# Pairs of blocks of the first MLP product by seven products: linear attention and a GELU MLP on one Trainium2 core

## The chip, the cores and the metric

The kernel runs on one core of one Trainium2 chip. The metric is the device time of one execution in microseconds (us). Each kernel was run several times; the median is given. One execution of each was also recorded by the hardware profiler, and all stretches inside the kernel come from that record. The engines are PE (TensorE, matrix products), ACT (ScalarE), DVE (VectorE), POOL (GpSimd) and SP (SyncE, which here only issues DMAs). Each engine works through its own instructions in the order in which the program gives them.

## What is computed

```python
# attention: q, k, v are [4, 8, 768, 64]; lam has one decay per head
for b in range(nb):                                   # blocks of the sequence
    intra = (q_b @ k_b.T * Dmask) @ v_b               # Dmask[i, j] = lam ** (i - j) for i >= j, else 0
    inter = (q_b * lam_pow) @ kv_state
    out_b = intra + inter
    kv_state = lam_block * kv_state + (k_b * rev_pow).T @ v_b
# MLP on x = attention's output, as [3072 tokens, 512]
h = x @ w_in                                          # w_in [512, 2048]
g = 0.5 * h * (1 + erf(h / sqrt(2)))
out = g @ w_out                                       # w_out [2048, 512]
```

## The kernel before

**Chunks and groups.** The sequence of 768 is cut into 6 blocks of 128. With 4 batches this gives 24 chunks; chunk n is block n // 4 of batch n % 4. Four chunks (one block of all batches) make a group of 512 tokens. While PE works on the MLP of group g, the attention of the four chunks of group g + 1 is slipped in between. `xT[g]` holds a group's attention output, transposed, as `x_t` [128, 4, 512] in bf16, one 128-row slice per input block.

**Attention of a chunk.** `begin` takes the loaded q, k and v; from chunk 8 on they are transposed by DMAs that SP issues (L192, L193), and v is scaled on POOL (`decay_v`, L167). `scores` (L195) multiplies k with q into two PSUM tiles `sc_ps`, one per half of the heads, and `masked` (L206) multiplies each by the mask on DVE into `sc_m` (L208). `outputs` (L226) adds the state's part and the chunk's own part into `o_ps`, which is then copied to `x_t`: on ACT for chunks below 8 (L243), on DVE from chunk 8 on (L245). `next_state` (L210) makes the next state with two DVE passes, an addition into `tmp` (L222) and a multiplication (L223). The loads of q, k and v are issued on POOL (L67), which also scales v.

**The MLP of group 0** has its own order. `mm1` (L407) makes one h block: four matmuls of 512 columns over the four input slices into `h_ps`, and a GELU on ACT into `g_t` (L420). `mm2` (L425) multiplies `g_t` with `w_out`, in two pairs of token blocks; each of the four results is copied by ACT into `o_sb` (L434, tag `o_s` of the output pool) and stored by SP (L435). The attention of chunks 4 to 7 stands in its second half: `transposes` on PE with ACT's copy of kT (L176), then `scores` and `outputs`.

**The MLP of groups 1 to 5.** The first stage is sixteen h blocks. The second stage is the product with `w_out`, done by seven products of halves in place of eight (`blocks_by_seven`, L271): `g_sum` (L280) builds five sums of halves of `g_t` on DVE, and m3, m4, m5, m2, m1, m6 and m7 each make one of the products, in two steps of eight matmuls of 256 columns (L310). Their results are combined on DVE and ACT into `o0` and `o1`, which SP stores (L320). In the last group the two halves of `r_ps` are two tiles, in banks of their own:

```python
if last:
    banks["r"] = [bank([128, DH], F32, tag, "r_ps") for tag in ("mh", "t")]
```

**PSUM.** There are eight banks. `bank` (L155) hands them out by tag: two each for `sc`, `mh` (h blocks, s, r) and `mo` (p, q and others), one each for `o` and `t`. A tile that gets the buffer of an earlier one waits until every reader of that one is done. The same holds for the pools in SBUF; `g_pool` and `out_pool` have two buffers per tag.

**The order.** It is written by hand: `tc.manual_schedule()` keeps the program's order on each engine. For groups 1 to 5 a list `todo` gives each attention step a place, counted in matmul columns (`place`, L547), and the loop at L598 runs a step before the first MLP block that begins at or behind its place.

Of the kernel before, what the change touches and what calls it, by code (L numbers as in the profile page):

```python
# [8 lines left out]
F32 = mybir.dt.float32  # L9
BF16 = mybir.dt.bfloat16  # L10
# [5 lines left out]
def kernel(  # L16
# [34 lines left out]
    g_pool = ctx.enter_context(tc.tile_pool(name="g", bufs=2))  # L51
    out_pool = ctx.enter_context(tc.tile_pool(name="outp", bufs=2))
# [55 lines left out]
    nc.vector.tensor_scalar(negj, pos, -1.0, None, op0=ALU.mult)  # L108
    dist = consts.tile([128, C], F32)
# [45 lines left out]
    def bank(shape, dtype, tag, name):  # L155
        return ps.tile(shape, dtype, tag=tag, name=name, bufs=2 if tag in ("sc", "mh", "mo") else 1)
# [38 lines left out]
    def scores(c):  # L195
        sc_ps = [bank([128, HP, C], F32, "sc", f"sc_ps{hi}") for hi in range(2)]
        for hp in range(HP):
            for hi in range(2):
                p = slice(hi * D, (hi + 1) * D)
                nc.tensor.matmul(sc_ps[hi][:, hp, :], c.kT[p, hp, :], c.qT[p, hp, :], start=True, stop=True)  # L200
        c.sc_m = work_pool.tile([128, HP, 2, C], BF16, tag="sc_m", name="sc_m")
        c.sc_ps = sc_ps
        for hi in range(2 if c.n > 0 else 0):
            masked(c, hi)

    def masked(c, hi):  # L206
        mask = decay[:, hi] if c.early else cmask[:, None, :].to_broadcast((128, HP, C))
        nc.vector.tensor_mul(c.sc_m[:, :, hi, :], c.sc_ps[hi], mask)  # L208

    def next_state(c):  # L210
        if c.sb == NB - 1:
            return
        kv_ps = bank([128, HP, 128], F32, "t", "kv_ps")
        for hp in range(HP):
            nc.tensor.matmul(kv_ps[:, hp, :], c.k[:, 2 * hp:2 * hp + 2, :], c.v_dec[:, 2 * hp:2 * hp + 2, :],  # L215
                             start=True, stop=True)
        new = work_pool.tile([128, HP, 128], BF16, tag="state_f", name="state", bufs=8)
        if c.sb == 0:
            nc.vector.tensor_mul(new, kv_ps, lam_blk)
        else:  # L220
            tmp = work_pool.tile([128, HP, 128], F32, tag="tmp", name="tmp")
            nc.vector.tensor_add(tmp, kv_ps, states[c.n])  # L222
            nc.vector.tensor_mul(new, tmp, lam_blk)  # L223
        states[c.n + M] = new

    def outputs(c, x_t, off, evacuate=True):  # L226
        o_ps = bank([128, HP, C], F32, "o", "o_ps")
        if c.sb > 0:
            for hp in range(HP):
                nc.tensor.matmul(o_ps[:, hp, :], states[c.n][:, hp, :], c.qT[:, hp, :],  # L230
                                 start=(hp == 0), stop=False, skip_group_check=True)
        v = c.v if c.early else c.v_dec
        for hi in range(2):
            for hp in range(HP):
                nc.tensor.matmul(o_ps[hi * D:(hi + 1) * D, hp, :], v[:, 2 * hp + hi, :], c.sc_m[:, hp, hi, :],  # L235
                                 start=(c.sb == 0 and hp == 0), stop=True, skip_group_check=True)
        c.x_o, c.o_ps = x_t[:, :, off * C:(off + 1) * C], o_ps
        if evacuate:
            empty_outputs(c)
# [30 lines left out]

    def blocks_by_seven(g, g_t, first):  # L271

        last = g == NG - 1
        TH = M * C // 2
        lo, hi = slice(0, TH), slice(TH, 2 * TH)
        gsum = {}
        G_SUMS = {6: (0, hi, 0, lo, ALU.subtract), 1: (0, lo, KH, hi, ALU.add), 2: (0, hi, KH, hi, ALU.add),
                  5: (0, lo, KH, lo, ALU.add), 7: (KH, lo, KH, hi, ALU.subtract)}

# [8 lines left out]
        n4 = KH // 2  # L288

        def with_sums(i, run):  # L290
            def both():
                run()
                if 10 <= i < 15:
                    g_sum((5, 2, 1, 6, 7)[i - 10], 0)
            return both

        paired = [kf for k in range(KH) for kf in (k, k + KH)]
        blocks = [(with_sums(i, first[kf][0]), first[kf][1]) for i, kf in enumerate(paired)]
# [9 lines left out]
        def product(i, u, o, begin):  # L308
            for k in range(KH):
                nc.tensor.matmul(o, left[i](k, slice(u * C, (u + 1) * C)), right[i](k),  # L310
                                 start=(begin and k == 0), stop=(k == KH - 1), skip_group_check=True)
# [4 lines left out]

        def store(rows, us, cols):
            b = slice(rows * 2 + us.start, rows * 2 + us.stop)
            dst = out_r[g, :, b, cols]
            nc.sync.dma_start(dst, sb["o0" if rows == 0 else "o1"][:, us, cols])  # L320

        both, every = slice(0, 2), slice(0, d_model)

        def m3(u):
            if u == 0:
                banks["p"] = bank([128, 2, DH], F32, "mo", "p_ps")
            product(3, u, banks["p"][:, u, :], u == 0)
            if u == 1:
                nc.scalar.copy(tile_f("e"), banks["p"])
                g_sum(5, n4)  # L330

        def m4(u):
            if u == 0:
                banks["q"] = bank([128, 2, DH], F32, "mo", "q_ps")
            product(4, u, banks["q"][:, u, :], u == 0)
            if u == 0:
                g_sum(2, n4)
            else:
                nc.scalar.copy(tile_f("f"), banks["q"])

        def m5(u):
            if u == 0:
                banks["p5"] = bank([128, 2, DH], F32, "mo", "p5_ps")
                g_sum(1, n4)
            product(5, u, banks["p5"][:, u, :], u == 0)
            if u == 1:
                sb["o0"] = out_pool.tile([128, 2, d_model], F32, tag="o0", name="o0_sb")
                nc.vector.tensor_add(sb["o0"][:, :, d_hi], sb["e"], banks["p5"])
                nc.vector.tensor_sub(tile_f("x1"), sb["f"], banks["p5"])
                if last:  # L350
                    store(0, both, d_hi)

        def m2(u):
            if u == 0:
                banks["q2"] = bank([128, 2, DH], F32, "mo", "q2_ps")
            product(2, u, banks["q2"][:, u, :], u == 0)
            if u == 0:
                g_sum(6, n4)
            else:
                sb["o1"] = out_pool.tile([128, 2, d_model], F32, tag="o1", name="o1_sb")  # L360
                nc.vector.tensor_add(sb["o1"][:, :, d_lo], sb["f"], banks["q2"])
                nc.vector.tensor_sub(tile_f("x2"), sb["e"], banks["q2"])

        def m1(u):
            if u == 0:
                banks["s"] = bank([128, 2, DH], F32, "mh", "s_ps")
                if last:
                    banks["r"] = [bank([128, DH], F32, tag, "r_ps") for tag in ("mh", "t")]
                else:
                    r_ps = bank([128, 2, DH], F32, "mh", "r_ps")  # L370
                    banks["r"] = [r_ps[:, 0, :], r_ps[:, 1, :]]
                    banks["r_all"] = r_ps
            product(1, u, banks["r"][u], u == 0 or last)
            if u == 0:
                g_sum(7, n4)
            elif last:
                for w in range(2):
                    nc.vector.tensor_add(sb["x2"][:, w, :], sb["x2"][:, w, :], banks["r"][w])
            else:
                nc.vector.tensor_add(sb["x2"], sb["x2"], banks["r_all"])  # L380

        def m6(u):
            product(6, u, banks["s"][:, u, :], u == 0)
            if u == 1:
                nc.vector.tensor_add(sb["o1"][:, :, d_hi], sb["x2"], banks["s"])
                store(1, both, every)

        def m7(u):
            product(7, u, banks["r"][u], False)
            if last:  # L390
                nc.vector.tensor_add(sb["o0"][:, u, d_lo], sb["x1"][:, u, :], banks["r"][u])
                store(0, slice(u, u + 1), d_lo)
            elif u == 1:
                nc.vector.tensor_add(sb["o0"][:, :, d_lo], sb["x1"], banks["r_all"])
                store(0, both, every)

        blocks += [((lambda f=f, u=u: f(u)), KH * DH) for f in (m3, m4, m5, m2, m1, m6, m7) for u in range(2)]
# [3 lines left out]

    def mlp_blocks(g):
        T = M * C
        x_t = xT[g]
        g_t = g_pool.tile([128, NK2, T], BF16, tag="g", name="g_t")
# [139 lines left out]
    later = NK2 * 4 * M * C + 7 * 2 * KH * DH  # L545

    def place(at):  # L547
        g, f = int(at), at - int(at)
        return round(f * total) if g == 0 else round(total + (g - 1 + f) * later)
# [11 lines left out]
        14: [lambda: next_state(live[3])],  # L561
        e: [w_out_sums, lambda: decay_v(live[4], nc.vector)],
# [12 lines left out]
    for n in range(2 * M, NCH):  # L575
# [4 lines left out]
                 (place(g + (at + apart if i < M - 1 else 0.93)), -OUTPUTS, n)]  # L580
# [3 lines left out]
    def step(minus_kind, n):  # L584
# [10 lines left out]
        else:  # L595
            outputs(live[n], xT[n // M], n % M)

# [45 lines left out]
```

## Time and profile before

| | |
|---|---|
| median of 3 runs (lowest to highest) | 211.31 us (211.16 to 211.94) |
| the profiled execution's own time | 211.0 us |
| its span, first to last instruction | 209.2 us |
| granted PE clock, mean | 0.997 |
| PE busy | 200.2 us (96%) |
| DVE busy | 139.8 us (67%) |
| ACT busy | 82.8 us (40%) |
| POOL busy | 94.8 us (45%) |
| PE's share of the chain that ended last | 92% |

The chain is the sequence of work and waits followed back from the last instruction. A row of the groups gives the line, engine, operation and shapes, then the total busy time, the mean in ns, and the idle time of the engine just before, with what ended most of it. The time of a matmul in such a row includes its way through the array, so consecutive matmuls overlap; how fast PE goes on is read from the chain or from the starts.

### The profile page before, as it was taken

How to read it: one execution, taken by the hardware profiler on the slowest of the kernel's cores; microseconds unless marked ns; L12 is line 12 of the kernel's file. 1: busy time of each engine (PE TensorE's matmuls, PEld its weight loads, DVE VectorE, ACT ScalarE, POOL GpSimd, SP SyncE). 2: the span in 40 equal slices, each digit the busy share in tenths (PEclk: the TensorE clock that was granted, in tenths of full speed). 3: DMA queues.
4: the chain of work that ended last, by engine and by line, in shares of the span. 5: the costliest groups of instructions: out<-in, count | busy, mean ns of one | idle time of the engine just before them, and what ended most of it. 6: DMA issues, size and time to landing. Idle time of an engine off the chain costs nothing.

```text
span 209.2 us, 4108 instructions
## 1 busy us (share of the span) xinstructions
PE 200.2 (96%) x1687; PEld 129.7 (62%) x1705; DVE 139.8 (67%) x220; ACT 82.8 (40%) x151; POOL 94.8 (45%) x110
## 2 busy tenths in 40 slices
PE   6689999999999999999999999999999999999992
PEld 1346674456545688655688655688654688544882
DVE  2583436665568889688779689579678579223382
ACT  4696664223556410255420265420265420366200
POOL 8978963899999793399500394000100000000000
PEclk9999999999999999999999999999999999999998
DMA  3999999999999999699990599100651000500014
GB/s 87 178 187 178 198 206 192 154 213 163 172 187 125 155 156 141 191 141 160 161 66 0 202 137 185 20 13 3 211 106 37 3 0 3 200 0 0 3 50 150
DMA packets 102370, 24.78 MB, mean 118 GB/s; under 512 B 92880, under 2 KB 99536, under 8 KB 102352
## 3 DMA queue, kind: packets, MB, share of 16 engines
q0 software_dynamic: 78096, 13.24, 90.3%
q1 hardware_dynamic: 23216, 11.02, 24.2%
q10 hardware_dynamic: 1040, 0.26, 0.6%
q8 instruction: 13, 0.21, 0.4%
q14 instruction: 5, 0.04, 0.1%
HBM read 27.27 MB, written 6.29 MB: 160 GB/s over the span
## 4 chain that ended last, share of the span: by engine, by line
PE 92%; DMA 3%; DVE 2%; issue 1%; ACT 1%; SPq 0%; DVEq 0%
PE h_ps L416 40%; PE r_ps L310 9%; PE p_ps L310 9%; PE q_ps L310 8%; PE o_ps L430 7%; PE o_ps L235 4%; PE s_ps L310 4%; PE sc_ps L200 4%; DMA wide_kq<-in_k_dram 3%; PE kv_ps L215 2%; PE o_ps L230 2%; PE t_ps L173 2%; DVE sc_m L208 1%; PE idle_ps L475 1%; DVE decay L496 0%
## 5 line engine op out<-in xcount | busy, mean ns | idle before, releaser
L420 ACT ACTIVATE g_t<-h_ps 128x512 bf16<-128x512 f32 (+3 forms) x101 | 58.1, 576 | 78.4 <-PE h_ps L416 78.2
L416 PE MATMUL h_ps<-x_t,w_in_t 128*128 128x512 bf16 (+3 forms) x434 | 88.5, 348 | 0.7
L416 PEld LDWEIGHTS <-w_in_t 128*128 128x128 bf16 x448 | 39.5, 98 | 36.2 <-issue 0.7
L167 POOL TENSOR_TENSOR v_dec<-v_t,lam_m 128x512 bf16<-128x512 bf16 x23 | 24.6, 1076 | 47.3 <-PE kv_ps L215 44.4
L310 PEld LDWEIGHTS <-g_sum 128*128 128x128 bf16 x400 | 38.5, 98 | 5.1
L285 DVE TENSOR_TENSOR g_sum<-g_t 128x1024 bf16<-128x1024 bf16 x50 | 34.0, 725 | 11.2 <-ACT g_t L420 11.2
L208 DVE TENSOR_TENSOR sc_m<-sc_ps,cmask 128x512 bf16<-128x512 f32 x40 | 25.6, 680 | 2.0 <-PE sc_ps L200 2.0
L67 POOL DMA_DIRECT2D k_t<-in_k_dram x23 | 21.2, 920 | 2.1 <-DMA w_out_t<-in_moe_w_out_dram 1.8
L67 POOL DMA_DIRECT2D q_t<-in_q_dram x23 | 20.5, 893 | 2.2 <-DMA w_out_t<-in_moe_w_out_dram 2.2
L67 POOL DMA_DIRECT2D v_t<-in_v_dram x23 | 20.4, 889 | 1.7 <-DMA w_out_t<-in_moe_w_out_dram 1.7
L310 PE MATMUL r_ps<-w_sum,g_sum 128*128 128x256 bf16 x160 | 19.3, 273 | 0.0
L310 PEld LDWEIGHTS <-g_t 128*128 128x128 bf16 x160 | 15.3, 98 | 3.2
L245 DVE TENSOR_TENSOR x_t<-o_ps,lam_q 128x512 bf16<-128x512 f32 x16 | 11.0, 687 | 8.4 <-PE o_ps L235 8.4
L222 DVE TENSOR_TENSOR tmp<-kv_ps,state 128x512 f32<-128x512 f32 x16 | 11.0, 689 | 7.3 <-PE kv_ps L215 7.3
L223 DVE TENSOR_TENSOR state<-tmp,lam_blk 128x512 bf16<-128x512 f32 x16 | 15.5, 972 | 0.5
L430 PE MATMUL o_ps<-w_out_t,g_t 128*128 128x512 bf16 x61 | 14.8, 380 | 0.1
L200 PE MATMUL sc_ps<-qT,kT 64*128 64x128 bf16 x192 | 10.0, 222 | 0.7 <-DVE sc_m L208 0.3
L200 PEld LDWEIGHTS <-kT 64*128 64x128 bf16 x192 | 5.8, 95 | 7.1 <-issue 2.7
L475 PE MATMUL idle_ps<-idle 128*128 128x512 bf16 x24 | 9.1, 495 | 1.2 <-DVE idle L101 1.2
L310 PE MATMUL p_ps<-w_sum,g_t 128*128 128x256 bf16 x80 | 10.1, 273 | 0.0
L310 PE MATMUL q_ps<-w_sum,g_t 128*128 128x256 bf16 x80 | 9.7, 273 | 0.0
L310 PE MATMUL q_ps<-w_out_t,g_sum 128*128 128x256 bf16 x80 | 9.6, 273 | 0.0
(67 smaller groups left out, 169.2 us busy)
## 6 DMA issues: line engine op xcount, KB each, us to landing
out_dram<-o_sb SPq DMA_DIRECT2D x9, 512.0 KB, 3.0
k_t<-in_k_dram POOLq DMA_DIRECT2D x23, 128.0 KB, 6.6
q_t<-in_q_dram POOLq DMA_DIRECT2D x23, 128.0 KB, 6.6
v_t<-in_v_dram POOLq DMA_DIRECT2D x23, 128.0 KB, 6.6
w_in_t<-in_moe_w_in_dram POOLq DMA_DIRECT2D x8, 256.0 KB, 8.7
w_out_t<-in_moe_w_out_dram POOLq DMA_DIRECT2D x4, 512.0 KB, 10.4
out_dram<-o_sb SPq DMA_DIRECT2D x5, 256.0 KB, 5.3
wide_kq<-in_q_dram ACTq DMA_DIRECT2D x1, 256.0 KB, 4.7
```

The source lines that it names most:

```text
L67: nc.gpsimd.dma_start(raw[n, name], chunk_of(name, n))
L167: eng.tensor_mul(c.v_dec, c.v, lam_m[:, :, None].to_broadcast((128, H, D)))
L200: nc.tensor.matmul(sc_ps[hi][:, hp, :], c.kT[p, hp, :], c.qT[p, hp, :], start=True, stop=True)
L208: nc.vector.tensor_mul(c.sc_m[:, :, hi, :], c.sc_ps[hi], mask)
L222: nc.vector.tensor_add(tmp, kv_ps, states[c.n])
L223: nc.vector.tensor_mul(new, tmp, lam_blk)
L285: nc.vector.tensor_tensor(gsum[i][:, ks, :], g_t[:, ka + k:ka + k + n4, ta], g_t[:, kb + k:kb + k + n4, tb], op=op)
L310: nc.tensor.matmul(o, left[i](k, slice(u * C, (u + 1) * C)), right[i](k), start=(begin and k == 0), stop=(k == KH - 1), skip_group_check=True)
L416: nc.tensor.matmul(h_ps[:, k, lo:hi], w_in_t[:, ki, (kf + k) * 128:(kf + k + 1) * 128], x_t[:, ki, cols.start + lo:cols.start + hi], start ...
L420: nc.scalar.activation(g_t[:, kf:kf + ks, cols], h_ps, ACT.Gelu)
L430: nc.tensor.matmul(om[io], g_t[:, kf, io * C:(io + 1) * C], w_out_t[:, kf, :], start=(kf == 0), stop=(kf == NK2 - 1))
L475: nc.tensor.matmul(idle_ps[0], idle[:, :128], idle, start=True, stop=True)
```

## The change

The change has five parts.

1. In groups 1 to 5, three (group 1) or four (the others) pairs of h blocks, kf and kf + 8, are made by seven products of halves, with 256 columns each, in place of sixteen half products. `pair_by_seven` gives two steps, `first` and `second`, with other blocks between them. Five sums of parts of `w_in` are made once on DVE (`w_in_sums`), and four sums of parts of `x_t` in each group (`x_sums`). Each pair has two banks of tag `mo`, `c_ps` and `d_ps`; ACT copies out of them, POOL adds, DVE subtracts and adds, and ACT's GELU reads c and the sum t.
2. From chunk 8 on, the scores of both halves lie in one tile of two banks; ACT copies them to bf16 and DVE multiplies by a bf16 mask in place.
3. The state's multiplication goes to POOL for blocks 2 to 4 of the sequence.
4. The seven products with `w_out` are ordered anew (m3, m4, m3, m4, m1, m6, m5, m2, m7), the later ones add onto the banks of the earlier ones, and POOL forms a common sum y.
5. `g_t` is one buffer for all groups, and the output pool has one buffer per tag. The last outputs of a group stand at 0.9 of it, not 0.93.

The core of the diff (bodies that are only re-sorted are left out):

```diff
-    g_pool = ctx.enter_context(tc.tile_pool(name="g", bufs=2))
-    out_pool = ctx.enter_context(tc.tile_pool(name="outp", bufs=2))
+    g_pool = ctx.enter_context(tc.tile_pool(name="g", bufs=1))
+    out_pool = ctx.enter_context(tc.tile_pool(name="outp", bufs=1))
...
+    cmask_b = consts.tile([128, C], BF16)
+    nc.vector.tensor_copy(cmask_b, cmask)
...
     def scores(c):
-        sc_ps = [bank([128, HP, C], F32, "sc", f"sc_ps{hi}") for hi in range(2)]
+        sc_ps = bank([128, 2, HP, C], F32, "sc", "sc_ps")
...
-        for hi in range(2 if c.n > 0 else 0):
-            masked(c, hi)
+        if c.n >= 2 * M:
+            nc.scalar.copy(c.sc_m, sc_ps)
+            flat = c.sc_m.rearrange("p hi hp i -> p (hi hp) i")
+            nc.vector.tensor_mul(flat, flat, cmask_b[:, None, :].to_broadcast((128, H, C)))
+        else:
+            for hi in range(2 if c.n > 0 else 0):
+                masked(c, hi)
...
-            nc.vector.tensor_mul(new, tmp, lam_blk)
+            (nc.vector if c.sb == 1 else nc.gpsimd).tensor_mul(new, tmp, lam_blk)
...
+    PAIRS = {g: 3 if g == 1 else 4 for g in range(1, NG)}
...
+    def w_in_sums():
+        for i, (a, b, op) in W_IN_SUMS.items():
+            wisum[i] = w_pool.tile([128, 2, SW * 128], BF16, name=f"wi_sum{i}")
+            nc.vector.tensor_tensor(wisum[i], w_in_t[:, a[0], a[1]], w_in_t[:, b[0], b[1]], op=op)
...
+    def x_sums(g):
+        x_t = xT[g]
+        both = sum_pool.tile([128, NK1, TH], BF16, tag="xs67", name="x_sum67")
+        for i, pa, pb, op in ((4, (d1, t_lo), (d0, t_lo), ALU.subtract), (3, (d0, t_hi), (d1, t_hi), ALU.subtract),
+                              (1, (d0, t_lo), (d1, t_hi), ALU.add)):
+            xsum[i] = sum_pool.tile([128, 2, TH], BF16, tag=f"xs{i}", name=f"x_sum{i}")
+            nc.vector.tensor_tensor(xsum[i], x_t[:, pa[0], pa[1]], x_t[:, pb[0], pb[1]], op=op)
+        nc.vector.tensor_tensor(both, x_t[:, :, t_lo], x_t[:, :, t_hi], op=ALU.add)
+        xsum[6], xsum[7] = both[:, d0], both[:, d1]
...
+        def product(i, o, begin, end=True):
+            for ki in range(2):
+                nc.tensor.matmul(o, w[i][:, ki, :], x[i][:, ki, :], start=(begin and ki == 0), stop=(end and ki == 1),
+                                 skip_group_check=True)
+
+        def first():
+            sb["c"] = bank([128, 2, TH], F32, "mo", "c_ps")
+            sb["d"] = bank([128, 2, TH], F32, "mo", "d_ps")
+            product(4, sb["c"][:, 1], True)
+            product(3, sb["c"][:, 0], False)
+            zf = sum_pool.tile([128, 2, TH], F32, tag="h_zf", name="h_zf", bufs=2)
+            nc.scalar.copy(zf, sb["c"])
+            product(1, sb["d"][:, 0], True)
+            e = sum_pool.tile([128, TH], F32, tag="h_e", name="h_e", bufs=2)
+            nc.scalar.copy(e, sb["d"][:, 0])
+            product(6, sb["d"][:, 1], False)
+            y = sum_pool.tile([128, TH], F32, tag="h_y", name="h_y", bufs=2)
+            nc.gpsimd.tensor_add(y, zf[:, 0], zf[:, 1])
+            nc.gpsimd.tensor_add(y, y, e)
+            sb["y"] = y
+
+        def second():
+            product(5, sb["c"][:, 0], False)
+            product(2, sb["c"][:, 1], False)
+            t = sum_pool.tile([128, 2, TH], F32, tag="h_t", name="h_t", bufs=2)
+            nc.vector.tensor_sub(t, sb["y"][:, None, :].to_broadcast((128, 2, TH)), sb["c"])
+            nc.scalar.activation(halves[:, 2 * kf + 1:2 * (kf + KH) + 1:2 * KH - 1, :], sb["c"], ACT.Gelu)
+            product(7, sb["d"][:, 0], True)
+            nc.vector.tensor_add(t, t, sb["d"])
+            nc.scalar.activation(halves[:, 2 * kf:2 * (kf + KH) + 2:2 * KH + 1, :], t, ACT.Gelu)
+        return (first, 8 * TH), (second, 6 * TH)
...
-        paired = [kf for k in range(KH) for kf in (k, k + KH)]
-        blocks = [(with_sums(i, first[kf][0]), first[kf][1]) for i, kf in enumerate(paired)]
+        seven = [None] + [pair_by_seven(g, kf, g_t) for kf in range(1, PAIRS[g] + 1)]
+        if g == 1:
+            order = [0, 8, 5, 13, (1, 0), 6, (1, 1), 14, (2, 0), 4, (2, 1), 12, (3, 0), 7, (3, 1), 15]
+        else:
+            order = [0, (1, 0), 8, (1, 1), 5, (2, 0), 13, (2, 1), 6, (3, 0), 14, (3, 1), 7, (4, 0), 15, (4, 1)]
+        blocks = [seven[o[0]][o[1]] if isinstance(o, tuple) else first[o] for o in order]
+        blocks[-2] = then(blocks[-2], 1, 0)
+        blocks[-1] = then(blocks[-1], 6, 0)
...
+        early_k, late_k = (0, 5, 6, 7), (1, 2, 3, 4)
+        def m3(part):
+            if part == 0:
+                two("p", "mo")
+                product(3, each("p"), True, False, early_k)
+                g_sum(1, n4)
             else:
+                product(3, each("p"), False, True, late_k)
+                nc.scalar.copy(tile_f("z"), banks["p"])
+                g_sum(5, 0)
...
+        def m2(u):
+            product(2, each("q"), False, us=(u,))
+            if u == 1:
+                tile_o(1)
+                nc.vector.tensor_sub(sb[1][:, :, d_hi], sb["y"], banks["q"])
+                nc.vector.tensor_add(sb[1][:, :, d_hi], sb[1][:, :, d_hi], banks["s"])
+                nc.scalar.copy(sb[1][:, :, d_lo], banks["q"])
                 store(1, both, every)
...
+        steps = [(m3, 0), (m4, 0), (m3, 1), (m4, 1)] + [(f, u) for f in (m1, m6, m5, m2, m7) for u in range(2)]
...
+    g_t = g_pool.tile([128, NK2, M * C], BF16, name="g_t")
...
+        e - 3: [w_in_sums],
         e: [w_out_sums, lambda: decay_v(live[4], nc.vector)],
...
-                 (place(g + (at + apart if i < M - 1 else 0.93)), -OUTPUTS, n)]
+                 (place(g + (at + apart if i < M - 1 else 0.9)), -OUTPUTS, n)]
...
             outputs(live[n], xT[n // M], n % M)
+            if n % M == M - 1:
+                x_sums(n // M)
```

More of the change, by code (lines that the diff above doesn't have):

```diff
@@ L234, in outputs @@
             for hp in range(HP):
[L235 removed]
+                nc.tensor.matmul(o_ps[hi * D:(hi + 1) * D, hp, :], v[:, 2 * hp + hi, :], c.sc_m[:, hi, hp, :],
                                  start=(c.sb == 0 and hp == 0), stop=True, skip_group_check=True)
@@ new lines, in pair_by_seven @@
+    def pair_by_seven(g, kf, g_t):
+        x_t = xT[g]
+        own = lambda f: slice(f * 128, (f + 1) * 128)
+        w = {3: w_in_t[:, d0, own(kf)], 4: w_in_t[:, d1, own(kf + KH)]}
+        w.update({i: wisum[i][:, :, own(kf - 1)] for i in W_IN_SUMS})
+        x = dict(xsum)
+        x.update({2: x_t[:, d0, t_lo], 5: x_t[:, d1, t_hi]})
+        halves = g_t.rearrange("p kf (th t) -> p (kf th) t", th=2)
+        sb = {}
+        def product(i, o, begin, end=True):
[27 more added lines that the diff above has]
+        return (first, 8 * TH), (second, 6 * TH)
@@ L306, in blocks_by_seven, with product, two @@
         banks, sb = {}, {}
[L308 to L311, printed above, removed]
+        def product(i, o, begin, end=True, ks=range(KH), us=(0, 1)):
+            for k in ks:
+                for u in us:
+                    nc.tensor.matmul(o[u], left[i](k, slice(u * C, (u + 1) * C)), right[i](k),
+                                     start=(begin and k == ks[0] and u == us[0]), stop=(end and k == ks[-1]),
+                                     skip_group_check=True)
+        def two(name, tag):
+            banks[name] = bank([128, 2, DH], F32, tag, f"{name}_ps")
+            return banks[name]
+        each = lambda name: [banks[name][:, u, :] for u in range(2)]
         def tile_f(name):
@@ L353, in m2 @@
         def m2(u):
[L354 to L380, printed above, removed]
```

107 lines of the change are left out of this document (62 added, 45 removed).

## The prediction

> **What bounds the kernel now.** I read the page first: which engine is full, and when.
>
> ```profile
> PE 200.2 (96%) x1687; PEld 129.7 (62%) x1705; DVE 139.8 (67%) x220; ACT 82.8 (40%) x151; POOL 94.8 (45%) x110
> PE   6689999999999999999999999999999999999992
> ```
>
> PE is full from the third slice to the last. A change gains only if it shortens PE's stream and leaves PE waiting for nobody. Next, the chain of waits, once for group 2 and once for group 5, gives the stage before the w_out products.
>
> ```profile
> 86.12 0.22 PE h_ps L416
> ...
> 102.28 0.87 PE p_ps L310 x8
> ```
> ```profile
> 179.40 0.21 PE h_ps L416
> ...
> 193.29 1.75 PE p_ps L310 x16
> ```
>
> So that stage takes 16.16 us in group 2 (groups 3 and 4 alike) and 13.89 in group 5, which has no attention: 16 h blocks of 0.868. Sixteen 256-column matmuls take 1.75, 0.109 each. Group 1's stage, from the full chain, is 54.83 to 71.19: 16.36.
>
> Third, the groups by form, for what the new evacuations cost.
>
> ```profile
> L420 ACT ACTIVATE g_t<-h_ps 128x512 bf16<-128x512 f32 x86 | 51.4, 597 | 74.8 <-PE h_ps L416 74.8
> L329 ACT COPY f_e<-p_ps 128x512 f32<-128x512 f32 x5 | 2.9, 586 | 9.0 <-DVE sc_m L208 6.6 <-PE p_ps L310 2.3
> L420 ACT ACTIVATE g_t<-h_ps 128x256 bf16<-128x256 f32 x3 | 1.2, 384 | 0.1
> L167 POOL TENSOR_TENSOR v_dec<-v_t,lam_m 128x512 bf16<-128x512 bf16 x23 | 24.6, 1076 | 47.3 <-PE kv_ps L215 44.4 <-DMA v_t<-in_v_dram 2.4 <-PE h_ps L416 0.4
> ```
>
> Fourth, the timeline at two places, for the gaps between engines.
>
> ```profile
> 40.05 0.59 ACT L434 COPY o_sb<-o_ps 128x512 f32<-128x512 f32 x1 [5.45 <-PE o_ps L430]
> 40.67 1.22 SPq L435 DMA_DIRECT2D out_dram<-o_sb  x2
> 40.92 0.59 ACT L434 COPY o_sb<-o_ps 128x512 f32<-128x512 f32 x1 [0.28 <-PE o_ps L430]
> 41.40 0.59 ACT L176 COPY kT<-t_ps 128x512 bf16<-128x512 bf16 x1
> 42.18 0.40 PE L200 MATMUL sc_ps<-qT,kT 64*128 64x128 bf16 x8
> ```
> ```profile
> 54.87 0.59 ACT L243 CAST x_t<-o_ps 128x512 bf16<-128x512 f32 x1 [0.20 <-PE o_ps L235]
> 55.73 0.39 PE L215 MATMUL kv_ps<-v_dec,k_t 128*128 128x128 bf16 x4
> 55.95 0.59 PE L416 MATMUL h_ps<-x_t,w_in_t 128*128 128x512 bf16 x2
> 56.15 0.69 DVE L222 TENSOR_TENSOR tmp<-kv_ps,state 128x512 f32<-128x512 f32 x1 [1.75 <-PE kv_ps L215]
> ```
>
> ACT starts one 512-wide piece 0.48 after another (40.92, 41.40). A reader of PSUM starts 0.20 after PE has gone on (55.95, 56.15). An engine's result reaches the next engine in about 0.05 (DVE's qT ends at 42.13, the scores start at 42.18). DVE's state multiply, which needs tmp, starts 0.72 after it (58.97, 59.69).
>
> **The saving.** Each of 19 pairs (3 + 4x4) replaces two h blocks (1.736) by 14 matmuls (1.53): 0.21 each, 3.9 us.
>
> **What a pair waits for.** Call its halves A (`first`) and B (`second`). In A, ACT copies bank c (`zf`), then half of bank d (`e`); product 6 writes d's other half. No row of before shows a reader and PE in one bank: in group 5, where DVE reads one half of r_ps while PE writes the other, L368 puts them in two banks. So either product 6 waits for `e` or it doesn't. I take the wait, since `d_ps` is one tile of one bank. Likewise Gelu of c behind DVE's subtraction from c. From c's last matmul: 0.20 + 0.48 + 0.38 + 0.06 = 1.12 until product 6, where PE's own work is 0.22 (product 1).
>
> The Trainium skill, page "PSUM — Partial Sum Buffer", section "PSUM bank collisions raise a hardware error", says that no two engines may be in one bank and quadrant at once, two readers included. By it both waits are there, 256 us; without them it is the first rival, 233. The split r_ps agrees, but shows no wait.
>
> ACT, in order, then closes a ring: product 6 0.22, h block 0.87, products 5 and 2 0.44, gap 0.20, subtraction 0.72, addition 0.69, gap 0.05, Gelu of t 0.48, Gelu of the next h block 0.48, `zf` 0.48, `e` 0.38, gap 0.06: **5.07 us per pair**, where four blocks took 3.47. GpSimd's two adds make y beside it: at half of 1.08 each they end 0.59 + 0.05 + 1.08 = 1.72 after `zf` starts, and the subtraction starts at 2.65. At a full 1.08 each they come 0.2 late, 3.8 in all; cheaper adds gain nothing.
>
> Group 5: first block and A up to product 6: 0.87+0.44+0.20+0.48+0.38+0.06+0.22 = 2.65; three rings 15.21; then, since p_ps takes c's bank, block 15, products 5 and 2, gap, subtraction, Gelu of c and two gaps: 0.87+0.44+0.20+0.69+0.05+0.60+0.05 = 2.90. Sum 20.76, so +6.9.
>
> Groups 2 to 4 add attention. Two kv products on the ring's path: 0.44. The masks: ACT's copy of 1024, an estimate from 384 and 586 for 256 and 512, is 1.01, then DVE's multiply 0.60, both ahead of the subtraction. Scores ahead of h block 8: 0.33+0.20+1.01+0.05+0.60 = 2.19 instead of 1.51, +0.68; with outputs (0.57) ahead of block 14: +1.25. Sum 23.13 against 16.16: +7.0 each, **21.0**. Off the ring, the copy would be free.
>
> Group 1: four blocks and two kv 3.91, A 1.78, two rings 10.14, a kv 0.22, a score copy in ACT's queue 0.9, then 2.76 to the last subtraction and 1.39 to p_ps: 21.10 against 16.36, +4.7. Together the pair stages cost **32.6**, the saving included.
>
> **The output pool with one buffer.** Tag `o_s` has it too. Group 0's second output copy must wait until the first's store has landed:
>
> ```profile
> DMA to landing us min/median/max: 5.3/5.5/6.1
> ```
>
> 40.67 + 5.5 = 46.2. Behind it in ACT's queue is kT, at 46.7 to 47.2, and PE's scores for chunk 4 go from 42.18 to 47.3: 5.1 us. The other two copies do it again: the store of the third, issued near 53.4 + 5.1, lands at 64.0; behind the fourth is x_t of chunk 7 (54.87), which group 1's first h block needs: 65.1 instead of 60.6, 4.6 us. Together **9.7** (9.3 to 10.9 by the landings).
>
> PE then stands still for longer than it took to lose its clock at the end, where its last matmuls end near 205.5 (the windows; the column behind the busy times is the granted clock):
>
> ```profile
> 207.60:208.20 0.60, 0.00 (x0) 0.00 (x0) 0.00 (x0) 0.00 (x0) 0.00 (x0) 0.79 0.02 3
> 208.20:208.80 0.60, 0.00 (x0) 0.00 (x0) 0.00 (x0) 0.00 (x0) 0.00 (x0) 0.50 0.00 0
> ```
>
> At the start a 512 took 0.43 from 7.7 until about 10, then 0.22. Three us at half speed lose 1.5: **3.0** for two gaps (0 to 3.4).
>
> **What costs nothing.** w_in sums: five of 0.69 on DVE ahead of w_out's, where DVE waits 1.85 and 1.99 for w_out; uncovered, 3.4. x sums, 1.95 per group, have most of 2.6 us behind the last outputs; uncovered, up to 1.3. The mask copy hides in DVE's 4.2 us wait for k. State decay on GpSimd (near 1.08, row L167) is needed a group later; ahead of y it fits into 0.9 of slack. The loads (0.9 each) go out ahead of the next pair's adds. Outputs at 0.9 still stand before m7. g_t's single buffer is read by g_sums that m7 itself waits for. The w_out stage keeps its 112 matmuls; DVE's work there (eight g_sums 5.4, three x_t and two masks 3.5, four combinations 2.7, x sums 1.95: 13.5 of 14.9 us) stays ahead of the products, and a late g_sum would cost 0.68. The combinations in four steps save DVE three passes that were off PE's path; in the last group they put SP's store of o1 behind two DVE passes instead of one, 0.7 later, and its 3.0 us still land before the last store's (uncovered, 0.7).
>
> The Trainium skill, page "SBUF — State Buffer", section "Who interferes with whom", lets a DVE operation with two SBUF inputs contend with GpSimd's reads. L223 has two and took 0.69 to 1.39. By that rule eight masks could take 0.7 more each, 262 us. Subtraction and addition read PSUM and stay.
>
> **Sum.** 32.6 + 9.7 + 3.0 = 45.3 on the profiled execution's 211.0 (span 209.2, 1.8 around it; the median of 3 is 211.31): **256**.
>
> **Rivals.**
> 1. One bank is shared freely: no wait at product 6 or at Gelu of c. The ring becomes `zf` 0.59, gap, two adds 1.08, gap, 0.72, 0.69, gap, two Gelus 0.96: 4.19. Group 5 +2.7, groups 2 to 4 +2.0 each, group 1 +0.9, output pool 12.7: 233. For it: the halves are different addresses. 12%.
> 2. The output copies don't wait, though the pool says one buffer: 256 - 12.7 = 244. 7%.
> 3. Faster: evacuations stay hidden as Gelu is now (0.27 idle after each). It decides itself where ACT, GpSimd and DVE return both banks within a pair cycle's 3.27 us of PE work. Then 211.0 - 3.9 = 207. Against it: even the shorter ring is 4.19. 6%.
> 4. PE's clock falls in the pair stages, where it is busy 3.3 of 5.1 us: matmuls on the ring (1.53) double, 19 x 1.53 = 29, giving 285. Against it: no gap there reaches 2 us. 5%.
>
> The forecast has 70%, by itself 249 to 266 (dearer adds, contention; gaps a tenth shorter). The range reaches down to rival 1: 232 to 266. Measurement tells 0.5% from no change. Faster 0.05, same 0.01 (rest of rival 3), slower 0.94.
>
> **What would show it.** Right: PE idle before c_ps and d_ps, released by ACT's copy of `e` and Gelu of c; A some 2 us long; c_ps every 5 us; PE idle about 5 us near 42 and 4.6 near 60, behind o_sb's DMA; p_ps 20.8 us after group 5's first h block. Wrong: product 6 starting right behind product 1, kT right behind the second o_sb copy, or PE full through the pair stages.

## The result, and the profile after

The changed kernel takes **264.15 us** (median of 4 runs, 262.66 to 267.04) against 211.24 for the kernel before on the same chip: a ratio of 1.2472, 95% interval 1.2407 to 1.2537. The medians are of all runs, but the ratios leave out slow runs (here the one of 267.04), so that a ratio can differ a little from that of the medians. The profiled execution took 264.56, its span is 262.8. Line numbers below are those of the changed kernel, or of the experiment's, which differ by a few.

The page's busy totals and its row of slices for PE, and the clock granted to it:

```profile
PE 210.3 (80%) x1819; PEld 143.2 (55%) x1819; DVE 159.8 (61%) x240; ACT 120.8 (46%) x221; POOL 154.2 (59%) x170
...
PE   5899994798858898667899687599867599865893
...
PEclk9799999599989999999999979999979999999998
```

PE was full from the third slice on; now no h stage (the stage of the first MLP product) is, and the clock row dips at four places between the kernel's start and its end. PE's busy time is 10 us longer though its stream is shorter; part of it runs at half clock. GpSimd went from 94.8 us to 154.2.

The waits (engine, tile and line, what it waited for; us in total, times, longest):

```profile
PE d_ps L318 <- ACT h_e L330: 22.1, 19, 2.2
...
ACT o_sb L524 <- DMA out_dram<-o_sb: 7.7, 2, 5.6
PE c_ps L318 <- ACT g_t L342: 7.6, 13, 1.2
...
PE p_ps L391 <- ACT g_t L342: 6.5, 5, 1.6
PE sc_ps L202 <- ACT kT L178: 5.3, 2, 5.2
```

Product 6 waits for ACT's copy of `e` in each of the 19 pairs. In 13 of them the pair's first product waits for Gelu of the c of the pair before. The timeline of group 5 holds one whole ring, the closed loop of steps from one pair's subtraction to the next pair's (start, duration, engine, line, and in brackets the idle time before it and what ended it):

```profile
234.12 0.69 DVE L341 TENSOR_TENSOR h_t<-h_y,c_ps 128x512 f32<-128x512 f32 x1 [3.74 <-PE c_ps L318]
...
234.91 0.69 DVE L344 TENSOR_TENSOR h_t<-h_t,d_ps 128x512 f32<-128x512 f32 x1
...
235.63 0.63 ACT L345 ACTIVATE g_t<-h_t 128x512 bf16<-128x512 f32 x1 [0.19 <-DVE h_t L344]
...
236.64 0.58 ACT L327 COPY h_zf<-c_ps 128x512 f32<-128x512 f32 x1
237.11 0.39 ACT L330 COPY h_e<-d_ps 128x256 f32<-128x256 f32 x1
...
237.55 0.38 PE L318 MATMUL d_ps<-x_sum,wi_sum 128*128 128x256 bf16 x2 [1.24 <-ACT h_e L330]
...
239.33 0.69 DVE L341 TENSOR_TENSOR h_t<-h_y,c_ps 128x512 f32<-128x512 f32 x1 [3.74 <-PE c_ps L318]
```

From 234.12 to 239.33 is 5.21 us, of which PE's own work, at the spacing of its matmuls in the kernel before, takes 3.27. Subtraction, addition, Gelu of t, Gelu of the h block, `zf`, `e`, product 6, the h block, products 5 and 2: this is the ring that the prediction wrote down.

The timeline of group 0 shows the output pool's one buffer, at both places:

```profile
46.57 0.59 ACT L524 COPY o_sb<-o_ps 128x512 f32<-128x512 f32 x1 [5.60 <-DMA out_dram<-o_sb]
...
47.70 0.61 PE L202 MATMUL sc_ps<-qT,kT 64*128 64x128 bf16 x8 [5.18 <-ACT kT L178]
...
63.16 0.59 ACT L524 COPY o_sb<-o_ps 128x512 f32<-128x512 f32 x1 [2.12 <-DMA out_dram<-o_sb]
```

PE's first gap is 5.2 us, and the clock is at half from 46.0 to 52.8. At the second place the store had landed after 2.0 us, and PE lost 1.0.

Stage by stage, from the starts of the matmuls in the two traces: group 1's first h block comes 7.7 us later; the h stages of groups 1 to 5 are longer by 8.8, 8.2, 10.0, 9.6 and 7.4; group 1's w_out stage by 1.1; the end by 0.8. Together 53.6, the difference of the spans.

### The profile page after: what moved, and what is told of

Same layout as the page of the kernel before. It is cut to its first block, busy times and chain, and to the rows that moved or that the text cites. A ratio compares the mean times of both kernels' runs of the same rounds, so it can differ in the third digit from the quotient of the medians.

```text
span 262.8 us, 4592 instructions
## 1 busy us (share of the span) xinstructions
PE 210.3 (80%) x1819; PEld 143.2 (55%) x1819; DVE 159.8 (61%) x240; ACT 120.8 (46%) x221; POOL 154.2 (59%) x170
## 4 chain that ended last, share of the span: by engine, by line
PE 47%; ACT 14%; POOL 11%; DVE 11%; issue 10%; DMA 5%; SPq 0%; DVEq 0%; POOLq 0%; ACTq 0%
PE h_ps L506 13%; PE p_ps L391 5%; PE o_ps L520 5%; DVE h_t L341 5%; PE q_ps L391 4%; DVE h_t L344 3%; PE r_ps L391 3%; ACT h_zf L327 3%; PE d_ps L318 3%; POOL v_dec L169 3%; PE c_ps L318 3%; DMA out_dram<-o_sb 3%; ACT g_t L345 3%; PE o_ps L242 2%; DMA wide_v<-in_v_dram 2%
## 5 line engine op out<-in xcount | busy, mean ns | idle before, releaser
L506 PE MATMUL h_ps<-x_t,w_in_t 128*128 128x512 bf16 (+3 forms) x296 | 61.5, 344 | 1.4 <-ACT x_t L250 1.0
L510 ACT ACTIVATE g_t<-h_ps 128x512 bf16<-128x512 f32 (+3 forms) x63 | 35.2, 560 | 34.5 <-PE h_ps L506 34.3
L333 POOL TENSOR_TENSOR h_y<-h_zf 128x256 f32<-128x256 f32 x19 | 14.0, 735 | 45.8 <-ACT h_zf L327 45.8
L318 PE MATMUL d_ps<-x_sum,wi_sum 128*128 128x256 bf16 x114 | 22.4, 279 | 22.1 <-ACT h_e L330 22.1
L318 PEld LDWEIGHTS <-wi_sum 128*128 128x128 bf16 x190 | 19.1, 101 | 32.5 <-issue 27.1
L506 PEld LDWEIGHTS <-w_in_t 128*128 128x128 bf16 x296 | 25.5, 100 | 18.8 <-issue 4.1
L341 DVE TENSOR_TENSOR h_t<-h_y,c_ps 128x512 f32<-128x512 f32 x19 | 13.0, 685 | 27.2 <-PE c_ps L318 21.9
L206 ACT CAST sc_m<-sc_ps 128x1024 bf16<-128x1024 f32 x16 | 16.2, 1011 | 23.9 <-PE sc_ps L202 23.9
L230 POOL TENSOR_TENSOR state<-tmp,lam_blk 128x512 bf16<-128x512 f32 x12 | 15.3, 1271 | 17.3 <-DVE tmp L229 17.3
L342 ACT ACTIVATE g_t<-c_ps 128x512 bf16<-128x512 f32 x19 | 11.4, 598 | 18.5 <-DVE h_t L341 18.5
L208 DVE TENSOR_TENSOR sc_m<-sc_m,cmask_b 128x1024 bf16<-128x1024 bf16 x16 | 12.4, 776 | 12.2 <-ACT sc_m L206 12.2
L318 PE MATMUL c_ps<-x_sum,w_in_t 128*128 128x256 bf16 x76 | 11.4, 271 | 7.6 <-ACT g_t L342 7.6
L252 DVE TENSOR_TENSOR x_t<-o_ps,lam_q 128x512 bf16<-128x512 f32 x16 | 11.0, 685 | 10.6 <-PE o_ps L242 10.6
## 6 DMA issues: line engine op xcount, KB each, us to landing
w_out_t<-in_moe_w_out_dram POOLq DMA_DIRECT2D x4, 512.0 KB, 10.4
```

What stands on the lines that cost most here:

```text
L206: nc.scalar.copy(c.sc_m, sc_ps)
L230: (nc.vector if c.sb == 1 else nc.gpsimd).tensor_mul(new, tmp, lam_blk)
L318: nc.tensor.matmul(o, w[i][:, ki, :], x[i][:, ki, :], start=(begin and ki == 0), stop=(end and ki == 1), skip_group_check=True)
L333: nc.gpsimd.tensor_add(y, zf[:, 0], zf[:, 1])
L341: nc.vector.tensor_sub(t, sb["y"][:, None, :].to_broadcast((128, 2, TH)), sb["c"])
L506: nc.tensor.matmul(h_ps[:, k, lo:hi], w_in_t[:, ki, (kf + k) * 128:(kf + k + 1) * 128], x_t[:, ki, cols.start + lo:cols.start + hi], start ...
```

## The experiments

**1. Two output buffers.** The copies of group 0 use the two larger output tiles in turn (lines shortened at `...`):

```
-  o_sb = out_pool.tile([128, d_model], F32, tag="o_s", ...)
+  o_sb = out_pool.tile([128, 2, d_model], F32, tag=f"o{io % 2}", ...)[:, 0, :]
```

> Group 0's output copies take turns in two buffers (those of the later groups, which stand empty until then), everything else as after the change. Theory (the one buffer costs two gaps and PE's clock behind the first): the gap of 5.2 us ahead of the scores near 47.7 goes, so does the 1.0 us ahead of group 1's first h block, and the stretch at half speed behind the first gap (48.2 to 53, some 1.5 us); 264.2 falls by 7 to 8 us, to 256 to 257, and group 1's first h block comes near 55 instead of 62.4. Rival (the copies wait for something else, or the time is lost again in the pair stages): less than 3 us, 261 or more.

Measured: 253.59 us, 10.6 less (ratio to before 1.2027, 1.195 to 1.2103). Both waits are gone, and the first h block of group 1 comes at 55.70, 6.7 us earlier. The rest of the gain is in the h stages of groups 1, 3 and 4 (2.2, 1.8 and 1.4 shorter), where this execution had no stretch at half clock and the changed kernel's had one each; it had one in group 2, which is 1.1 longer. The 10.6 thus holds 6.7 from group 0 and a balance of half-clock stretches; why fewer of them came without the gaps isn't shown.

**2. No pairs.** `PAIRS` is 0 everywhere, all blocks plain, everything else as changed.

> All 16 h blocks of each group are plain again, in the order of the kernel before; the sums of w_in and of x are still made, and masks, state, combinations and the one output buffer stay as after the change. Theory (the pair stages cost 42 to 45 us, by the stage lengths of the trace: 8.8, 8.2, 10.0, 9.6 and 7.4, less what sums and masks cost by themselves): about 220 to 222, group 5's h stage 13.9 again, groups 2 to 4 near 16.2. Rival (masks on ACT, state on GpSimd and x sums are what stretches groups 2 to 4, and only group 5's 7.4 and group 1's part are the pairs'): 240 or more, with h stages of 20 or more in groups 2 to 4.

Measured: 232.19 us (1.0952, 1.0882 to 1.1023). Taking the pairs out gains 32.0 us, and the h stages of groups 2 to 4 are back at 16.16. So the rival is wrong on the h stages; but the time is 10 us above the upper end of what the theory gave, because the w_out stages of groups 1 to 4 became longer (17.69, 17.08, 17.08 and 16.10, after 16.08 and three times 14.9 with pairs) and group 1's h stage, with a wait for x_t and a stretch at half clock, stays at 20.62.

**3. Product 6 first.** In `first`, the copy of `e` and product 6 change places.

> In the first half of a pair, product 6 is issued ahead of ACT's copy of the other half of the same bank, so nothing holds it; the copy waits for it. Theory (PE's wait of 1.2 us for that copy lies on the ring that sets a pair's time): product 6, the h block and products 5 and 2 come 0.6 to 1.0 earlier per pair, the ring of 5.2 falls to 4.4 to 4.7, and 19 pairs give 10 to 15 us: 249 to 254. Rival (the wait is slack: the subtraction waits for y, from GpSimd, or ACT's queue sets the time): less than 3 us, and the subtraction's wait is now put down to GpSimd's adds.

Measured: 253.18 us, 11.0 less (1.2, 1.1935 to 1.2064). The timeline of group 5:

```profile
226.37 0.73 POOL L333 TENSOR_TENSOR h_y<-h_zf 128x256 f32<-128x256 f32 x1 [3.21 <-ACT h_zf L327]
...
227.17 0.73 POOL L334 TENSOR_TENSOR h_y<-h_y,h_e 128x256 f32<-128x256 f32 x1
...
227.93 0.69 DVE L341 TENSOR_TENSOR h_t<-h_y,c_ps 128x512 f32<-128x512 f32 x1 [3.27 <-POOL h_y L334]
```

The ring is 4.75 (subtractions at 218.44, 223.19, 227.93). The wait for `e` was on it; behind it stand GpSimd's two adds, and the subtraction now waits for them. Nineteen times 0.46 are 8.7 of the 11.0; the rest wasn't divided up.

**4. No pairs and two output buffers.**

> No pairs and two output buffers; bf16 masks, GpSimd's state decay, the sums of w_in and of x and the combinations in four steps stay. Theory (these parts are hidden beside PE, as the prediction costed them at nothing): 211 to 214. Rival (they cost by themselves, through GpSimd's slow passes, the shared port or a clock that falls): 216 or more, with PE idle ahead of outputs or h blocks.

Measured: 221.79 us (1.0493, 1.0457 to 1.0529): the rival. With this run the two causes are seen to add up: pairs cost 32.0 with one buffer and 31.8 with two, the buffer 10.6 with pairs and 10.4 without (by the ratios 32.1, 32.4, 9.4 and 9.7). 10.5 us are left over the kernel before. The timeline of group 2's end:

```profile
120.31 1.55 DVE L301 TENSOR_TENSOR x_sum<-x_t 128x512 bf16<-128x512 bf16 x3
121.78 0.68 DVE L302 TENSOR_TENSOR x_sum<-x_t 128x1024 bf16<-128x1024 bf16 x1
...
123.09 0.69 DVE L469 TENSOR_TENSOR o_sb<-o_sb,s_ps 128x512 f32<-128x512 f32 x1
...
123.83 1.02 PE L503 MATMUL h_ps<-x_t,w_in_t 128*128 128x512 bf16 x3 [1.44 <-DVE o_sb L469]
```

The x sums stand on VectorE ahead of the combination that empties the s bank, and the next group's first h block needs that bank: four such waits, 4.9 us.

**5. The same without any sums of w_in and x,** which nothing reads once there are no pairs.

> As the run without pairs and with two output buffers (221.8), and the sums of w_in and of x are left out, since nothing reads them there. Masks on bf16 copies, state decay on GpSimd and the combinations in four steps stay. Theory (the x sums stand on VectorE ahead of the three combinations that empty the s bank and the r bank, and PE's h block waits 1.2 to 1.4 us for that four times; the w_in sums delay the start): PE's waits behind the combination at the end of each w_out stage go, the stages after group 1's fall by 1.2 to 2, and the time is 213 to 215. Rival (GpSimd is what costs: its two passes of 1.6 us for y stretch VectorE's g_sums beside them from 0.69 to 1.6, so VectorE is late without the x sums too): 218 or more.

Measured: 214.82 us (1.0161, 1.0118 to 1.0203), 7.0 less, as the theory had it. The timeline of group 1's w_out stage shows what is left:

```profile
76.38 1.82 POOL L431 TENSOR_TENSOR f_y<-f_z,f_f 128x512 f32<-128x512 f32 x1 [8.79 <-ACT f_f L429]
76.39 4.03 DVE L362 TENSOR_TENSOR g_sum<-g_t 128x1024 bf16<-128x1024 bf16 x3
78.28 1.59 POOL L449 TENSOR_TENSOR f_y<-f_y,f_e 128x512 f32<-128x512 f32 x1
```

Three g_sums beside GpSimd's adds for y take 4.03; three in a row with GpSimd idle, at 71.84, took 1.90.

**6. Of the change only the four steps** (masks and state decay as before, no pairs, no sums, two buffers; the scores still lie in one tile of two banks).

> As the run without the sums, and masks and state decay are back as before the change: what is left of the change is the combinations in four steps and the last outputs at 0.9. Theory (VectorE is lighter by a pass of two masks and a state multiply moved to ScalarE and GpSimd only in name; these cost little either way): within 1 us of the run without the sums. Rival (GpSimd's state multiplies and the longer way of a mask through two engines hold outputs up, as the wait of 1.1 us of the outputs for the mask in that run says): 1 to 3 us below it, near 212.

Measured: 223.02 us, spread from 219.82 to 225.03 (1.0445, 1.0358 to 1.0532). Neither expectation: it is slower than experiment 5 by 8, and even its fastest run by 5. Its profile, of a run of 223.70, has h stages of 20.1 and 18.7 in groups 2 and 3, the scores waiting twice for a transpose of q (4.6 in all), and a stretch at half clock in group 2. Whether the shared score tile has a part in it, and why the transposes come late there, stays open, so this run doesn't price masks and state decay.

**7. Adds of y in a pair on VectorE,** with the edits of 1 and 3.

> The whole change with two output buffers and product 6 first, and the two adds that make y in a pair are on VectorE instead of GpSimd. Theory (with product 6 free the ring runs from zf through GpSimd's two adds, 0.72 and 0.73, to the subtraction; a VectorE add of 256 columns takes about 0.4 with its start): the ring falls from 4.75 to about 4.1, and with the two edits' own 10.5 and 11 the time is 228 to 235. Rival (VectorE, now with two more passes in each pair and the masks, becomes late): 240 or more, as with two output buffers and product 6 first alone (264.2 - 10.6 - 11.0 = 242.6).

Measured: 243.44 us (1.1505, 1.1447 to 1.1562). The ring is 4.19 (208.60, 212.79, 216.98), as expected, and group 5's h stage 17.94 instead of 19.39. But the time is the rival's: in groups 2 to 4, where VectorE has masks, kv sums (the two passes of `next_state`) and x_t as well, the stages fall only to 22.0. Two stretches at half clock add to it, one in group 1's h stage (from 66.5) and one in the last w_out stage (from 223.5), which is 18.49 long instead of 16.83.

**8. Gelu of t behind the next pair's copies,** added to 7 (the edit in short; a group's last pair keeps its Gelu of t in place).

```
-  nc.scalar.activation(<t's blocks>, t, ACT.Gelu)
+  pending.append(lambda: nc.scalar.activation(<t's blocks>, t, ACT.Gelu))
   # and in the next first(), behind the copies: pending.pop()()
```

> As the run with the adds on VectorE, and Gelu of t is issued on ScalarE behind the next pair's two copies instead of ahead of them. Theory (ScalarE's order closes the ring: addition, Gelu of t, Gelu of the h block, zf; without Gelu of t in it the ring goes subtraction 0.79, Gelu of c 0.65, products 4 and 3 0.64, zf 0.64, two adds 0.8): a ring of 3.5 to 3.7 and a further 6 to 9 us less, 221 to 228; group 5's stage 14.5 to 16. Rival (the ring is set elsewhere by then, by VectorE's four passes of a pair or by attention): less than 3 us.

Measured: 237.22 us (1.1206, 1.1169 to 1.1243), 6.2 less. The ring is 3.74 (205.64, 209.38, 213.12), group 5's stage 16.57; groups 2 to 4 stay at 21.6, so the total misses 221 to 228 while the ring comes close to its 3.5 to 3.7. Not all of the 6.2 is Gelu's: the last w_out stage is 1.6 shorter because the stretch at half clock of experiment 7 is not there, and group 1's h stage is 1.4 shorter, with its own gone as well. ACT's order was the last part of the ring that the prediction named.

**9. Spaced pairs.** The kernel before with two pairs in groups 2 to 5 (A3 and B3 are the halves of pair 3; g_t and the output tiles as in experiment 4; the edit in short):

```
+  order = [0, 8, 1, A3, 9, 2, B3, 10, 5, A4, 13, 6, B4, 14, 7, 15]
+  # x sums behind block 0; Gelu of t behind the h block that follows B
```

> The kernel before, with two pairs in each of groups 2 to 5 and more work between their halves: A, two h blocks, B, two h blocks, A, and so on; product 6 first, y on VectorE, Gelu of t one h block later, the x sums behind group's first h block, the w_in sums (two pairs' worth) spread over group 1; masks, state and combinations as before the change. Theory (the pairs cost only because their evacuations close a ring longer than PE's work between them; the last run's ring of 3.74 misses PE's 3.27 by little): with two h blocks more per pair nothing waits, each of 8 pairs saves 0.21, and the time is 209.5 to 210.5 against 211.2. Rival 1 (the bank waits stay, or VectorE is late with masks beside the pairs' four passes): 212 to 216. Rival 2 (the x sums hold the combinations up again): PE idle at the start of the h stages, 1 us each.

Measured: 225.18 us (1.0655, 1.0606 to 1.0703), slower than the first rival. In groups 2 to 4 VectorE is late: in group 3, y stands behind masks and a kv sum, and a subtraction whose bank was ready near 132.0 stands behind two more kv sums and starts at 133.81. Group 5 is the exception: with 2 pairs and 12 blocks its stage is 14.12, with one wait of PE, 0.48: a g_sum stands ahead of the second pair's subtraction (204.34, its bank ready near 203.9), and ACT's GELUs run late behind it.

**10. Adds of y in the w_out products on VectorE,** added to 5.

> As the run without the sums (214.8), and the two adds of y in the w_out products are on VectorE instead of GpSimd. Theory (the 3.3 us that are left over the kernel before come from GpSimd's two passes of 1.6 to 1.8: beside them VectorE's g_sums take 1.39 instead of 0.65, and outputs, masks and x_t come late behind them): g_sums beside the w_out products fall to 0.7, PE's waits for x_t (1.2) and for the masks (1.1) go, and the time is 211.5 to 212.5, though VectorE has two passes more. Rival (VectorE is simply too full there, or GpSimd's v_dec does the same): 214 or more.

Measured: 212.28 us (1.005, 1.0029 to 1.0071), 2.5 less. The group of g_sums in experiment 5 and here (total, mean ns):

```profile
L362 DVE TENSOR_TENSOR g_sum<-g_t 128x1024 bf16<-128x1024 bf16 x50 | 43.3, 923 | 22.0 <-ACT g_t L507 22.0
...
L362 DVE TENSOR_TENSOR g_sum<-g_t 128x1024 bf16<-128x1024 bf16 x50 | 32.9, 700 | 22.0 <-ACT g_t L507 22.0
```

The mean of a g_sum falls from 923 ns to 700, the w_out stages are 14.94 again, and the waits of PE's outputs for x_t and masks are gone, though VectorE has ten passes more.

**11. w_in sums alone,** added to 5.

> As the run without the sums, and the five w_in sums are made again; the x sums stay left out. It splits the 7.0 us that both kinds of sums cost there. Theory (the x sums, ahead of the combinations four times, cost 5 to 6 of it; the w_in sums, in a stretch where VectorE waits for w_out, cost 0 to 1.5): 215 to 216.3. Rival (the w_in sums delay the w_out sums and all behind them): 218 or more.

Measured: 215.00 us (1.0169, 1.0138 to 1.0201). The w_in sums cost 0.2 here, within what the runs differ; so 6.8 of the 7.0 are the x sums.

**12. Spaced pairs in group 5 only.**

> As the run with spaced pairs, but only group 5, which has no attention, takes its two pairs by seven products; groups 1 to 4 have plain blocks, and one g_sum of group 5 is issued behind the second pair's subtraction instead of ahead of it. Theory (with cover for every evacuation a pair saves its 0.21): group 5's h stage falls from 13.89 to 13.45 to 13.5, nothing else moves, and the time is 0.3 to 0.5 us below the kernel before, a ratio of 0.998. Rival (some wait is left in the pair, or the w_in sums in group 1 and the x sums cost what the pairs save): a ratio of 1.000 or more, group 5's stage 13.9 or longer.

Measured: 211.15 us against 211.33, a ratio of 0.9999 (0.998 to 1.0018): no difference. Group 5's stage is 13.60 instead of 13.89, so two pairs save 0.29 of the 0.42 that their matmuls are shorter by; the h stages of groups 2 to 4 are 0.09 longer each, which takes it back. What these 0.09 are wasn't followed. No version here beats the kernel before.

## Why the prediction came out as it did

**Pairs, 32.6 predicted: 32.0 measured** by taking them out. By group, experiment 1 against experiment 4 (h and w_out stage together): 4.6, 7.2, 6.1, 7.1 and 7.2, where the prediction had 4.7, 7.0 three times and 6.9. The mechanism was right: the ring's terms agree one by one: subtraction 0.79 and addition 0.72 with their starts (0.72 and 0.69 in the sum), Gelu of t 0.54 and of the h block 0.47, `zf` 0.47, `e` with its gap 0.44, product 6, the h block and products 5 and 2 1.51, then 0.27: 5.21 for 5.07. The choice that product 6 waits for `e` decided this, and rival 1, which had no such wait, is out: the wait stood in all 19 pairs. The Trainium skill, page "PSUM — Partial Sum Buffer", section "PSUM bank collisions raise a hardware error", has no two engines in a bank and quadrant at once; this kernel's order agrees (1.24 us between products 1 and 6 while ACT reads the other half), though a wait doesn't show what would happen without it.

The agreement in size is partly luck. Without pairs the x sums' wait comes to the surface at the stage's end; with them it doesn't (the w_out stages of groups 2 to 4 stay at 14.94). So the 32.0 is what pairs cost, less about 7 us of other waits that they hide. The prediction's own terms were lengths of h stages against the kernel before, and by these it was too low: with two buffers (experiment 1) the five are 6.6, 9.3, 8.2, 8.2 and 7.4 longer, 39.8 in all for 32.6. Group 5 took 21.27 for 20.76, mostly since the ring is 5.21 and not 5.07; attention then added 3.1 in groups 3 and 4 where the sum had 2.37; group 1 took 22.85 for 21.10; group 2 holds a stretch at half clock. Pairs without x sums can't be had, so how much of this the x sums are wasn't tried.

**GpSimd's adds: mis-sized.** At "half of 1.08 each" they were to be done well ahead of the subtraction. The groups by form, mean ns behind the comma:

```profile
L333 POOL TENSOR_TENSOR h_y<-h_zf 128x256 f32<-128x256 f32 x19 | 14.0, 735 | 45.8 <-ACT h_zf L327 45.8
...
L434 POOL TENSOR_TENSOR f_y<-f_z,f_f 128x512 f32<-128x512 f32 x5 | 6.9, 1385 | 22.8 <-ACT f_f L432 22.8
```

A first add takes 735 ns for 256 columns, a second 794 on average. In group 5 that still fits. In groups 2 to 4 the subtraction waits for y four times, up to 0.7 us (2.5 in all), and each time a state decay of 1.27 to 1.28 stands ahead of y on GpSimd, where the prediction had 1.08. The step "ahead of y it fits into 0.9 of slack" failed there.

**Output pool, 9.7 and 3.0 for the clock: 10.6 measured.** The first gap was right (5.2 for 5.1). The second was mis-sized: the store landed 2.0 us after its issue, not 5.5, so 1.0 instead of 4.6. Group 1's first h block comes 7.7 later, 6.2 of it from the gaps and 1.5 from the clock, where the prediction had 12.7. No row had shown the three us at half speed that it put behind each gap. Behind the start, the trace has five stretches of 3.4 us at half clock: two at the first gap, none at the second, and three inside pair stages (from 76.7, 151.8 and 192.8). That the whole came out near 10.6 is luck: the clock's cost in the pair stages, which the prediction gave nothing, took the place of the second gap. It is rival 4's mechanism, but for single stretches and not for all matmuls of the ring: between the changed kernel and experiment 1, an h stage is 1.1 to 2.2 longer where it holds one. Its ground against, "no gap there reaches 2 us", was no protection. Rival 2 is out, since both copies waited for the store.

**What costs nothing: this step failed.** 10.5 us, in three parts. (The w_in sums, 0.2, are as it said.) The x sums, 6.8 without pairs: the prediction gave them "2.6 us behind the last outputs" and up to 1.3, and added up VectorE's work in the stage (13.5 of 14.9), but asked only whether sums and products come in time, not what is queued behind them on VectorE: three combinations, one of which frees the bank of the next h block. The adds of y in the w_out products, 2.5: on GpSimd they were left out of the sum because they were off PE's path, and they stretched VectorE's g_sums. The remaining 1.0 (212.28 against 211.31) holds masks, state decay, the four steps and the longer end; by the stage lengths the end alone is 0.7, which the prediction named as uncovered.

The Trainium skill, page "SBUF — State Buffer", section "Who interferes with whom", says that a VectorE operation with two SBUF inputs contends with GpSimd's reads. The trace agrees, but not where the prediction put it: the masks on bf16 took 0.78 on average, by 0.18 more than the 0.60 of the sum, while g_sums, with two SBUF inputs as well, went from a mean of 725 ns to 966.

**The sum.** 32.0 for pairs, 10.6 for the buffer with its clock, 10.5 for the rest: 53.1, and 52.9 measured. These are steps between runs from one kernel to the other, so that they close says nothing by itself. Against the prediction's 45.3, the stretches of the trace say more: up to group 1's first h block it was 5.0 too dear (12.7 for 7.7), on the h stages 11.4 too cheap (32.6 for 44.0, of which some 4 are half clock by the comparison with experiment 1), and the rest, at nothing, was 1.9. Errors of both signs partly cancel, and the time came out 8 us above the forecast.

## What to carry to other kernels

Price each new pass by what stands behind it in its engine's queue as well as by who reads its result: an operation with time to spare for its own reader can hold the pass that frees a bank. When fewer matmuls are bought with more evacuations (copies out of PSUM), write the ring from one bank's release to the next in full, in each engine's order of issue; if it is longer than PE's work in it, the saving is gone, and moving one link (product 6, the adds, Gelu of t) only brings up the next: 5.21, 4.75, 4.19, 3.74. Work moved to an idle GpSimd wasn't free for VectorE here.

## What the runs showed of the hardware that was not expected

The clock falls without any long gap. In these traces it changes on a grid of 3.41 us (in the changed kernel's, 151.8 is 22 such steps behind 76.7, and 192.8 another 12). Worked out from the matmul records of all fourteen traces on that grid (some records can be missing, so the shares are good to a few per cent): steps at full clock in which PE was busy up to 40% were followed by a step at half clock; those with 50% or more were not; between 41 and 49% both happened. The windows of the changed kernel, one step with no fall behind it and one ahead of a fall (columns PE, PEld, DVE, ACT, POOL, clock, DMA):

```profile
203.00:206.40 3.40, 1.75 (x11) 0.88 (x10) 2.20 (x4) 2.40 (x6) 0.09 (x1) 1.00 0.00 0
148.40:151.80 3.40, 1.38 (x9) 0.75 (x8) 1.97 (x3) 2.08 (x4) 3.39 (x5) 1.00 0.90 108
```

PE is busy 1.38 of 3.40 ahead of the fall at 151.8, and 1.75 where nothing follows; its longest pause there was 1.2 us. The Trainium skill, page "TensorE: Matmul & The Clock Gate", section "What's actually happening", has a free-running window of about 3.4 us, with which the grid agrees, and puts the fall behind an idle window; here a window needn't be without work, since ahead of the three falls in the pair stages PE was busy 37, 41 and 46% of it.
